# First filter block in two halves of its channels, identity loaded apart, k and v in four pieces each, and a new written-out order

## The chip, the cores and the metric

The kernel runs on one core of a Trainium2 chip. A time is device microseconds (us) of one execution; the median of several runs counts. One more execution was taken by the hardware profiler. Engines: PE (TensorE matmuls), PEld (its weight loads), DVE (VectorE), ACT (ScalarE), POOL (GpSimd), SP (SyncE, which issues most DMAs).

## The reference

S = 2048, D = 640, F = 1728, bf16 inputs and output.

```python
def _A_ref(q, k, v, shift_k, ssm_k, ssm_D):          # q is the layernorm of A_q
    k_shift = causal 4-tap filter of k along S, per channel
    kv = k_shift * v
    y = irfft(rfft(kv padded to 2S) * rfft(ssm_k padded to 2S))[:S]   # a long convolution
    y = y + kv * ssm_D
    return q * y
def _B_ref(x, w1, b1, w2):
    h = x @ w1 + b1
    return (h * tanh(softplus(h))) @ w2               # Mish
x = A_q
h = x + _A_ref(layernorm(x), A_k, A_v, ...)
out = h + _B_ref(layernorm(h), B_w1, B_b1, B_w2)
```

## The kernel before

The long convolution is done as a Fourier transform of length 4096 in two steps of matmuls, 128 and 16 points, for the filter (`h`) and for the data (`x`), a product of the two, and the two steps back. Channels stand in five chunks `dc` of 128; a step's work is cut into blocks of one pair of PSUM banks (1024 columns of f32), each evicted to SBUF by one copy on ACT or DVE.

Names of the steps, with their lines before:

- `d_kn{dc}` (L206) loads chunk `dc` of the filter, 128 channels by 2048, 512 KB. `consts` (L196, L197) loads, on ACT's queue, one table of 106 KB (identity 128 columns, first Fourier matrix `fcfs` 256, a mask and a small identity 40) and then the row of `ssm_D` ("D row", `Drow`).
- `pewarm` (L239) and `pewarm2` (L258) are matmuls on zeros, 512 columns each, eight and two. `drow` (L245) turns the D row into a column with five one-column matmuls, and `dadd` (L268) adds it to the first time step of the filter.
- `k1pe{dc}` (L295): 16 PE transposes of a filter chunk; `k1ev{dc}_{0,1}` two copies out of the bank.
- `s1pe_h_{dc}_{0..3}` (L280): first Fourier step of the filter, 16 matmuls a block; `s1ev_h` its eviction. `s1pe_x`, the same for the data.
- `gb` (L251) builds the second Fourier matrix from the table R (`d_R`, L208). `s2pe_h_*`, `s2pe_x_*` (L363): second step, `s2ev` its eviction.
- `d_k0`, `d_k1` (L225) load k in two halves of 1280 KB, `d_v0`, `d_v1` (L228) load v. `ktpe{dc}_{h}` (L314) transposes k, `ktev` evicts; `shpe{dc}` (L333) is the 4-tap filter as matmuls, `kv` (L341) multiplies by v on DVE.
- `d_sw` (L382) moves a filter spectrum block across partitions by DMA, 256 KB. `pr` (L412) multiplies the spectra on DVE. `i1pe` (L423, L424) and `i2pe` (L485) are the steps back, `i1ev` and `yev` their evictions.
- Rows: `ln1_T` (L464, L465) statistics of row tile T; `ln1s` (L470, L471 on POOL) and `ln1f` (L473) their finish; `lnx` (L535 on ACT); for the first two tiles `wbA`, `hA`, `bnA` (L500, L502, L503) and `wbB`, `hB`, `bnB` (L504, L506, L509 to L511); for later ones `wb`, `h`, `ln2` (L517, L519, L523); `dr` (L541); then a PE transpose (`trpe`, L549, evicted by `trev`) for tiles 0 and 1, a DMA transpose (`d_tr`, L553) for the others.
- `m1pe{u}_{fc}` (L573, L576), `mi` (Mish on ACT, L580), `m2pe{T}` (L597), `res` (L605, L616) and `d_o` (L600) are the feed-forward part, in row blocks `u` of 1, 1, 2, 4, 4, 4 tiles.

Every copy out of PSUM is recorded at one line, L185. Each engine runs its queue in order; the order over all engines is written out in `ORDER`, one word a step: name, engine, bank slot, and for DMAs on SP `@name`, the copy behind which the load is paced. Waits between steps follow from the data and the banks. The head of `ORDER` before:

```
d_kn0:sp consts:act small:pool warmset:dve d_kn2:sp pewarm:pe:0 tab:act d_kn4:sp d_kn1:sp d_kn3:sp d_k0:sp d_R0:sp
d_k1:sp d_R1:sp drow:pe:0 d_v1:sp pewarm2:pe:1 dadd0:dve k1pe0:pe:1 d_v0:sp k1ev0_0:dve k1ev0_1:dve s1pe_h_0_0:pe:3
```

Of the kernel before, what the change touches and what calls it, by code (L numbers as in the profile page):

```python
# [10 lines left out]
ALU = mybir.AluOpType  # L11
# [158 lines left out]
def plan(v):  # L170
# [24 lines left out]
    def e_consts(e):  # L195
        v.nc.scalar.dma_start(v.consts[:], v.dram["consts"])  # L196
        v.nc.scalar.dma_start(v.buf("Drow", [P, D])[0:1], v.A_D.rearrange("(o d) -> o d", o=1))  # L197
    g.op("consts", "act", e_consts, w=["consts", "Drow"], kind="consts")
# [6 lines left out]
    for dc in range(NDC):  # L205
        dma(f"d_kn{dc}", 524e3, lambda e, dc=dc: v.nc.sync.dma_start(v.buf("kn", [P, NDC, S])[:, dc, :], v.A_h[dc * P:(dc + 1) * P, :]), w=[("kn", dc)])  # L206
# [16 lines left out]
    if KPE:  # L223
        for h in range(2):
            dma(f"d_k{h}", 2048 * KC, lambda e, h=h: v.nc.sync.dma_start(  # L225
                v.buf("kna", [P, NT, KC])[:, 8 * h:8 * h + 8, :], v.A_k[0].rearrange("(p a) d -> p a d", a=NT)[:, 8 * h:8 * h + 8, 0:KC]), w=[("kna", h)])
    for h in range(2):
        dma(f"d_v{h}", 1.31e6, lambda e, h=h: v.nc.sync.dma_start(  # L228
            v.buf("v", [P, NT, D])[:, 8 * h:8 * h + 8, :], v.A_v[0].rearrange("(p a) d -> p a d", a=NT)[:, 8 * h:8 * h + 8, :]), w=[("v", h)])
# [6 lines left out]
    def e_pewarm(e):  # L236
        pw = bank(wrt)
        for i in range(8):
            v.nc.tensor.matmul(pw[:, 0:512], v.buf("warm", [P, 512])[:, 0:128], v.buf("warm", [P, 512]), start=True, stop=True)  # L239
# [6 lines left out]
    g.op("drow", "pe", e_drow, r=["Drow", "consts"], allocs=[drt], kind="drow")  # L246
# [9 lines left out]
    def e_pewarm2(e):  # L256
        for i in range(2):
# [3 lines left out]
    keep = g.op("pewarm2", "pe", e_pewarm2, r=["warm"], allocs=[wrt2], kind="pewarm2", after=[o for o in g.ops if o.name == "drow"])  # L261
# [4 lines left out]
    for i, (c0, c1) in enumerate(((0, 1), (1, 2), (2, 5))):  # L266
# [21 lines left out]
    def k1(dc, grp):  # L288
        rt = alloc(D2)
        kk = f"kk{dc % 4}"  # L290

        def pe(e):
            pk = bank(rt, BF16).rearrange("p (t d) -> p t d", t=NT)
            for t2 in list(range(1, NT)) + [0]:
                v.nc.tensor.transpose(pk[:, t2, :], v.buf("kn", [P, NDC, S])[:, dc, t2:S:NT], v.ident)  # L295
        g.op(f"k1pe{dc}", "pe", pe, r=[("kn", dc), "consts"], allocs=[rt], kind="k1pe", after=[keep])
        for h in range(2):
            g.op(f"k1ev{dc}_{h}", EV, lambda e, h=h: ev(
                e, v.buf(kk, [P, 64, NT, 2])[:, 32 * h:32 * h + 32], bank(rt, BF16).rearrange("p (t d m) -> p d t m", t=NT, m=2)[:, 32 * h:32 * h + 32]),
                w=[(kk, h)], uses=[rt], kind="evb", arg=1024)  # L300
        s1("h", dc, lambda: v.buf(kk, [P, 64, NT, 2]), kk, f"B{grp}", GRP_DG[grp][0])
# [6 lines left out]
    for h in range(2):  # L308
        for dc in range(KPE):
# [5 lines left out]
            g.op(f"ktpe{dc}_{h}", "pe", pe, r=[("kna", h), "consts"], allocs=[rt], kind="ktpe")  # L315
# [216 lines left out]
    def rows(T):  # L532
# [11 lines left out]
        if T < NEAR:  # L544
# [5 lines left out]
            g.op(f"trpe{T}", "pe", pe, r=[hc, "consts"], allocs=[rt2], kind="trpe")  # L550
# [264 lines left out]
```

## Time and profile before

| | us |
|---|---|
| median of 3 runs (228.5 to 228.97) | 228.62 |
| the profiled execution | 230.95 |
| its span, first to last instruction | 229.2 |
| PE, DVE, ACT, POOL busy in the span | 215.5, 149.0, 139.4, 28.1 |

Durations of single steps come from the profiled execution. A step that is "busy" overlaps its neighbours on the same engine by some tens of ns, so a queue's pace is read from start to start. The page's 40 slices are 5.73 us each. A PE that is shown busy need not run at its full rate: the pitch of its matmuls tells that. "Landing" of a DMA is the time from issue until its semaphore tells of the end.

### The profile page before, as it was taken

The page shows a single profiled execution, that of the slowest core. Times are in us where ns is not written, and L with a number is a line of the kernel's source. Part 1 is how long each engine was busy: PE and PEld are TensorE (multiplying, and loading weights), DVE is VectorE, ACT ScalarE, POOL GpSimd, SP SyncE. Part 2 cuts the span into 40 slices and gives each one's busy share as a digit, 9 for nine tenths or more (in the row PEclk, how much of TensorE's full clock was granted, in tenths as well). Part 3 has the DMA queues.
Part 4 walks back from the last instruction along what each step waited for, and adds up shares of the span by engine and source line. Part 5 has one row for each costly group of instructions (what it writes and reads, how often), then busy time and mean ns, then how long its engine had stood idle before and what let it go on. Part 6 is the DMA issues. An engine that isn't in the chain of part 4 may idle for free.

```text
span 229.2 us, 6927 instructions
## 1 busy us (share of the span) xinstructions
PE 215.5 (94%) x3016; PEld 162.4 (71%) x3021; DVE 149.0 (65%) x274; ACT 139.4 (61%) x200; POOL 28.1 (12%) x60
## 2 busy tenths in 40 slices
PE   6899998979888999999999999999999999999994
PEld 2798888868787899998978764447557444577773
DVE  0469999999999999999999999965001200004131
ACT  2159998847999999999939367781350466100000
POOL 2120000000010000221233443522000000000000
PEclk9999999999999999999999999999999999999999
DMA  6999604845665777788230423424000100002021
GB/s 204 402 370 374 247 3 97 182 100 139 157 152 138 209 202 219 227 228 257 83 86 4 104 39 87 87 59 60 30 0 29 57 3 0 0 0 85 33 80 35
DMA packets 19872, 27.87 MB, mean 122 GB/s; under 512 B 10881, under 2 KB 14978, under 8 KB 19330
## 3 DMA queue, kind: packets, MB, share of 16 engines
q1 hardware_dynamic: 19536, 27.32, 41.0%
q8 instruction: 23, 0.38, 0.7%
q10 hardware_dynamic: 146, 0.11, 0.5%
q0 software_dynamic: 160, 0.01, 0.2%
q14 instruction: 7, 0.06, 0.1%
HBM read 17.27 MB, written 2.62 MB: 87 GB/s over the span
## 4 chain that ended last, share of the span: by engine, by line
PE 65%; ACT 14%; DVE 12%; DMA 4%; issue 3%; ACTq 0%; DVEq 0%
PE banks L597 26%; PE banks L573 23%; ACT arena L185 14%; PE banks L280 4%; DVE arena L412 4%; PE banks L363 3%; DVE arena L185 3%; PE banks L295 2%; DMA arena<-arena 2%; PE banks L333 2%; DMA arena<-in_A_ssm_D_dram 2%; DVE st L464 2%; DVE arena L341 2%; PE banks L576 1%; PE banks L485 1%
## 5 line engine op out<-in xcount | busy, mean ns | idle before, releaser
L185 ACT CAST arena<-banks 128x1024 bf16<-128x1024 f32 (+3 forms) x93 | 79.9, 985 | 16.5 <-PE banks L280 11.7
L597 PE MATMUL banks<-arena 128*128 128x320 bf16 (+2 forms) x448 | 61.7, 299 | 0.0
L580 ACT ACTIVATE arena<-banks,b1s 128x512 bf16<-128x512 f32 (+2 forms) x84 | 41.5, 535 | 29.7 <-PE banks L573 29.1
L573 PE MATMUL banks<-arena 128*128 128x512 bf16 (+2 forms) x395 | 58.2, 305 | 0.6 <-DVE nmr L473 0.3
L597 PEld LDWEIGHTS <-arena 128*128 128x128 bf16 x448 | 43.2, 98 | 18.1
L573 PEld LDWEIGHTS <-arena 128*128 128x128 bf16 x400 | 33.1, 98 | 23.7 <-issue 0.6
L616 DVE TENSOR_TENSOR arena<-banks,arena 128x640 bf16<-128x640 f32 x15 | 12.2, 816 | 56.4 <-PE banks L597 52.6
L185 DVE CAST arena<-banks 128x1024 bf16<-128x1024 f32 (+1 forms) x27 | 30.4, 1158 | 2.0 <-PE banks L280 1.3
L280 PE MATMUL banks<-consts,arena 128*64 128x128 bf16 x640 | 23.3, 230 | 2.6 <-ACT arena L185 1.1
L363 PE MATMUL banks<-arena 128*128 128x64 bf16 (+1 forms) x512 | 22.5, 199 | 2.7 <-ACT arena L185 2.4
L280 PEld LDWEIGHTS <-arena 128*64 128x64 bf16 x640 | 20.3, 116 | 4.7 <-issue 2.7
L363 PEld LDWEIGHTS <-arena 128*128 128x128 bf16 x512 | 19.9, 98 | 4.7 <-issue 3.6
L412 DVE TENSOR_TENSOR arena<-arena 128x2048 bf16<-128x2048 bf16 x20 | 22.9, 1216 | 0.2 <-DMA arena<-arena 0.2
L535 ACT ACTIVATE arena<-arena,nmr,r1v 128x640 bf16<-128x640 bf16 x16 | 14.3, 930 | 8.7 <-DVE nmr L473 7.5
L423 PE MATMUL banks<-a,arena 128*128 128x128 bf16 x160 | 18.8, 219 | 0.7 <-ACT arena L185 0.6
L424 PE MATMUL banks<-a,arena 128*128 128x128 bf16 x160 | 18.7, 219 | 0.0
L424 PEld LDWEIGHTS <-arena 128*128 128x128 bf16 x160 | 15.6, 98 | 0.9 <-issue 0.8
L423 PEld LDWEIGHTS <-arena 128*128 128x128 bf16 x160 | 15.6, 98 | 0.6 <-DVE arena L412 0.3
L185 DVE COPY arena<-banks 128x1024 bf16<-128x1024 bf16 (+1 forms) x17 | 10.7, 658 | 5.3 <-PE banks L295 4.5
L464 DVE BATCH_NORM_STATS2 st<-arena 128x6 f32<-128x320 bf16 x32 | 13.8, 474 | 0.0
L341 DVE TENSOR_TENSOR arena<-banks,arena 128x512 bf16<-128x512 f32 x20 | 12.3, 681 | 0.7 <-PE banks L333 0.3
L523 DVE BATCH_NORM_STATS2 st<-arena 128x6 f32<-128x320 bf16 x28 | 12.3, 480 | 0.2
(60 smaller groups left out, 139.6 us busy)
## 6 DMA issues: line engine op xcount, KB each, us to landing
arena<-arena SPq DMA_DIRECT2D x20, 256.0 KB, 3.0
arena<-in_A_ssm_k_dram SPq DMA_DIRECT2D x5, 512.0 KB, 6.4
arena<-in_A_k_dram SPq DMA_DIRECT2D x2, 1280.0 KB, 13.1
arena<-in_A_v_dram SPq DMA_DIRECT2D x2, 1280.0 KB, 19.6
arena<-in_A_q_dram SPq DMA_DIRECT2D x8, 320.0 KB, 3.2
out_dram<-arena SPq DMA_DIRECT2D x15, 160.0 KB, 1.8
arena<-in_B_w_dram SPq DMA_DIRECT2D x5, 432.0 KB, 4.4
arena<-in_B_w_dram SPq DMA_DIRECT2D x3, 480.0 KB, 5.1
```

Source lines behind the costliest of these rows:

```text
L185: v.copy = v.nc.scalar.copy(o, i) if e == "act" else v.nc.vector.tensor_copy(o, i)
L280: v.nc.tensor.matmul(pz[64 * ri:64 * ri + 64, gl, :], lhs, v.fcfs[:, ri, :], start=True, stop=True)
L341: v.nc.vector.tensor_tensor(v.buf(f"kvb{dc}", [P, 64, NT, 2])[:, q * 16:(q + 1) * 16], bank(rts[h])[:, i * 512:(i + 1) * 512].rearrange("p ...
L363: v.nc.tensor.matmul(bank(rt)[:, fl * pitch:fl * pitch + nd], v.buf("G", [P, P, P])[:, f0 + fl, :], v.buf(f"B{grp}", [P, P, nd])[:, f0 + f ...
L412: v.nc.vector.tensor_tensor(kk, xx.unsqueeze(1).to_broadcast([P, 2, 16, 64]), kk, ALU.mult)
L423: v.nc.tensor.matmul(pz[:, gl, :], v.buf(f"KP{b}", [P, 16, P])[:, 8 * h + gl, :], v.a12[:, 0, :], start=True, stop=False)
L424: v.nc.tensor.matmul(pz[:, gl, :], v.buf(f"KPS{b}", [P, 16, P])[:, 8 * h + gl, :], v.a12[:, 1, :], start=False, stop=True)
L464: v.nc.vector.bn_stats(v.st1[:, T % 4, q, :], x(T)[:, q * 320:(q + 1) * 320])
L535: g.op(f"lnx{T}", "act", lambda e: v.nc.scalar.activation(lnx(), x(T), ACT.Identity, scale=v.r1v[:, T:T + 1], bias=v.nmr1[:, T:T + 1]), r= ...
L573: v.nc.tensor.matmul(ph[:, 0:w], w1[:, dc, fc * P:(fc + 1) * P], lt[:, dc, T0 * P:T0 * P + w], start=(dc == 0), stop=(dc == NDC - 1))
L580: g.op(f"mi{u}_{fc}", "act", lambda e, fc=fc, rt=rt, ww=ww: v.nc.scalar.activation(ub()[:, fc, 0:ww], bank(rt)[:, 0:ww], ACT.Mish, bias=v. ...
L597: v.nc.tensor.matmul(bank(rt)[:, q * 512:q * 512 + b - a], lhs, w2()[:, wc, a:b], start=(fc == 0), stop=(fc == NFC - 1))
```

## The change

- The identity (128 columns of `consts`) is loaded by a DMA of its own, first on ACT's queue; then the D row, then the remaining 296 columns.
- `kn` chunk 0 is loaded in two halves of 64 channels. Its transposes become two groups, `k1pe0_0` and `k1pe0_1`, of 16 transposes on 64 rows each, in one bank each, with one copy each. For this chunk the D row is added behind the copy, on one partition (`dk0_0`, `dk0_1` on DVE), in place of the first `dadd`.
- `pewarm` has seven matmuls for eight, `pewarm2` one for two, and stands behind `pewarm` in place of `drow`.
- k and v are loaded in four pieces each (640 KB). These loads, R's and `a12` are paced behind copies, where they stood unpaced at the head.
- `ORDER` is another one throughout.

```diff
-        v.nc.scalar.dma_start(v.consts[:], v.dram["consts"])
         v.nc.scalar.dma_start(v.buf("Drow", [P, D])[0:1], v.A_D.rearrange("(o d) -> o d", o=1))
+        v.nc.scalar.dma_start(v.consts[:, 128:424], v.dram["consts"][:, 128:424])
+    g.op("ident", "act", lambda e: v.nc.scalar.dma_start(v.consts[:, 0:128], v.dram["consts"][:, 0:128]), w=["ident"], kind="ident")
...
-    for dc in range(NDC):
+    for h in range(2):
+        dma(f"d_kn0_{h}", 262e3, ... kn[64 * h:64 * h + 64, 0, :] <- A_h[64 * h:64 * h + 64, :] ...)
+    for dc in range(1, NDC):
...
-        for h in range(2):
-            dma(f"d_k{h}", 2048 * KC, ... [:, 8 * h:8 * h + 8, :] ...)
-    for h in range(2):
-        dma(f"d_v{h}", 1.31e6, ... [:, 8 * h:8 * h + 8, :] ...)
+        for h in range(4):
+            dma(f"d_k{h}", 1024 * KC, ... [:, 4 * h:4 * h + 4, :] ...)
+    for h in range(4):
+        dma(f"d_v{h}", 655e3, ... [:, 4 * h:4 * h + 4, :] ...)
...
-        for i in range(8):          # pewarm
+        for i in range(7):
-        for i in range(2):          # pewarm2
+        for i in range(1):
...
+        if dc == 0:
+            for h in range(2):
+                rt = alloc(D1)
+                def pe(e, h=h, rt=rt):
+                    pk = bank(rt, BF16).rearrange("p (t d) -> p t d", t=NT)
+                    c = slice(64 * h, 64 * h + 64)
+                    for t2 in range(NT):
+                        v.nc.tensor.transpose(pk[:, t2, :], v.buf("kn", [P, NDC, S])[c, 0, t2:S:NT], v.ident[c, c])
+                g.op(f"k1pe0_{h}", "pe", pe, r=[("kn", (0, h)), "ident"], ...)
+                g.op(f"k1ev0_{h}", EV, ...)
+                g.op(f"dk0_{h}", "dve", ... kk[0:1, half h, 0, :] += Drow[0:1, 64 * h:64 * h + 64] ...)
```

The head of the new order, and where its k, v and R loads stand:

```
ident:act d_kn0_0:sp small:pool warmset:dve consts:act d_kn0_1:sp pewarm:pe:0 d_kn1:sp tab:act d_kn4:sp d_kn3:sp d_kn2:sp
pewarm2:pe:0 k1pe0_0:pe:1 k1pe0_1:pe:2 k1ev0_0:dve drow:pe:3 dk0_0:dve k1ev0_1:act s1pe_h_0_0:pe:1 dadd0:dve s1pe_h_0_1:pe:0
s1ev_h_0_0:act k1pe1:pe:2 s1ev_h_0_1:dve k1ev1_0:act d_R0:sp:@s1ev_h_0_0 dk0_1:dve diag:dve s1pe_h_0_3:pe:1 s1ev_h_0_3:act
s1pe_h_1_1:pe:0 k1ev1_1:dve s1pe_h_1_3:pe:2 s1ev_h_1_1:act ...
d_k1:sp:@s1ev_h_1_1 d_v0:sp:@k1ev3_0 d_R1:sp:@s1ev_h_1_0 d_k0:sp:@k1ev4_0 d_v1:sp:@s2ev_h_0_1 d_v3:sp:@s1ev_h_4_3
d_k2:sp:@s1ev_h_3_2 d_k3:sp:@s2ev_h_0_4 d_v2:sp:@ktev1_0 d_a12:sp:@ktev0_0
```

Around the end of the products the DVE queue is `... pr_8_1 pr_8_0 ln1_1 ln1_0 ln1f_0 i1ev9_0 wbA0 hA0 bnA0 wbB0 hB0 bnB0 wbA1 yev2_1 dr0 ln1_2 trev0 ln1_3 hA1 bnA1 wbB1 ln1f_2 hB1 bnB1 yev2_0 wb3 dr1 wb2 h3 trev1`, where before it was `... pr_9_1 yev1_0 yev0_0 wbA1 wbA0 hA0 hA1 bnA1 bnA0 wbB0 hB0 bnB0 wbB1 hB1 bnB1 dr0 ln1_2 dr1 trev0 ln1_7 ln1_8 ln1_3 ln1_5 trev1`, with `ln1_0` and `ln1_1` some 30 us ahead, among the evictions of `s2pe_x`. `d_x2` and `d_x4` (row tiles 4, 5, 8, 9 of A_q) stand behind `yev2_0` and `yev2_2`.

## The prediction

> **What bounds the kernel now.** I read the page first, then the chain of waits, then busy time by stretches and the timeline.
>
> ```profile
> PE 215.5 (94%) x3016; PEld 162.4 (71%) x3021; DVE 149.0 (65%) x274; ACT 139.4 (61%) x200; POOL 28.1 (12%) x60
> DVE  0469999999999999999999999965001200004131
> ACT  2159998847999999999939367781350466100000
> ```
>
> The 65% of DVE is an average: it is full in slices 4 to 26 (17 to 150 us) and nearly idle after. So three stages are costed apart: to the last product (L412), from there to the second row block (L573), and the dense matmuls behind.
>
> ```profile
> 8.20:94.30 86.10, 78.33 (x1973) 72.26 (x1972) 80.38 (x100) 74.56 (x87) 5.19 (x9) 1.00 0.67 195
> 94.30:108.80 14.50, 13.97 (x204) 12.94 (x201) 13.69 (x39) 14.50 (x28) 2.48 (x5) 1.00 0.82 242
> ```
>
> Columns: stretch, length, busy PE, PEld, DVE, ACT, POOL. In stage 1 DVE is busy 80.4 of 86.1 us: evictions and products pace it. In stage 2 DVE is busy 13.7 of 14.5. Behind 108.8 PE hardly waits (from 109 to 229.2 it is busy 116.5 of 120.2 us, and the rest is nearly all the last 4.2 us), its work is the same in both versions, and each us at 108.8 is a us at the end.
>
> The head, from the chain of waits, then the timeline:
>
> ```profile
> 1.12 4.14 DMA arena<-in_A_ssm_D_dram
> 5.32 0.28 PE banks L245 x5
> 5.60 0.97 PE banks L258 x2
> 6.57 1.72 PE banks L295 x16
> 8.31 0.70 DVE arena L185
> 9.06 3.62 PE banks L280 x64
> ```
> ```profile
> 1.18 3.59 PE L239 MATMUL banks<-arena 128*128 128x512 bf16 x8 [1.18 <-DVE dumm L201]
> 5.32 0.28 PE L245 MATMUL banks<-consts,arena 1*128 1x1 bf16 x5 [0.54 <-DMA arena<-in_A_ssm_D_dram]
> ```
>
> The D row's load holds `drow`, then come `pewarm2`, `k1pe0`, one DVE copy, and the first filter block at 9.06. Last, L295 alone, by stretches (length, busy PE and PEld with counts, clock, DMA share, GB/s):
>
> ```profile
> 12.60:13.40 0.80, 0.79 (x8) 0.79 (x9) 1.00 0.97 319
> 13.40:14.20 0.80, 0.80 (x15) 0.80 (x14) 1.00 1.07 185
> ```
>
> 8 transposes in 0.8 us, then 15: PE runs at half speed until 13.4, though the clock column reads 1.00 throughout. L280 says the same: 64 in 3.62 us (0.90 per block of 16) up to 12.7, against 32 in 0.90 (0.45 a block) between 16.8 and 17.7.
>
> **Part by part.** The profiled execution took 230.95, its span 229.2 and 1.75 around it; the median of the runs is 228.62. The terms are made against the 229.2 span and carried over to the median as differences.
>
> *Head.* `pewarm` starts at 1.18, one per 0.427 us (the L239 weight loads stand at 2.01, 2.44, 2.86). Seven and `pewarm2`'s one keep PE busy to 1.18 + 8 x 0.427 = 4.60. `k1pe0_0` waits for the identity (the 106 KB table landed 3.9 us after 0.72, at 4.6; 32 KB of it, first on the same queue, is no later) and for half of `kn` 0 (the first whole one took 4.4 us, to 5.1; half its packets end earlier, 4.4 to 4.7). So it starts near 4.7 with a gap of about 0.1. Its 16 transposes move 64 columns, not 128: between 0.053 each (half of 1.72/16) and 0.107; I take 0.06, as the 64-column L363 matmuls also run at half the L295 pitch. That is 1.0, then 0.2 for the last write, 0.70 for the copy, 0.16 for `dk0_0` (the L268 add) and 0.1 of handoff: first block at 6.85 instead of 9.06, 2.2 earlier (bounds 1.4 and 2.4). The second half hides behind the copy; `drow` has 0.28 in the same shadow, and its D row (5.27 before) stands ahead of the big table now. `fcfs`, the 76 KB rest, must land before 6.85: the first 106 KB took from about 2.0 to 4.6, so 76 KB behind 4.5 take 1.9, to 6.4; if later, that is the loss. ACT's third issue (0.37) hides before its first copy at 6.8; so do five more issues on SP.
>
> 2.2 us at half speed are 2.4 blocks; later a block costs what ACT and DVE need together, 1/(1/0.90 + 1/1.15) = 0.50. Worth: 1.2.
>
> *The clock.* Before, the 3.59 us stretch from 1.18 did not raise it, nor the one from 5.32 to 8.29; the stretch from 9.06, with one gap of 0.2, did, 4.3 us on. The new stream stands from 1.18 to beyond 10 with gaps near 0.1, so the same 4.3 gives 5.5; I take 5.5 to 8.5. The Trainium skill, "TensorE: Matmul & The Clock Gate", Part 1, says that a free-running window of about 3.4 us must be busy throughout; by that the stretch from 1.18 raises the clock between 4.6 and 8.0; that 3.59 us did not suffice before agrees, as it would have had to meet a window almost exactly. From 6.85 the new PE queue holds five blocks and one `k1pe` up to 13.1 at half speed (5 x 0.90 + 1.72 = 6.2); at full speed 3.3, but their copies on ACT (five at 0.90 = 4.5) then bind: 4.5 in place of 6.2 to 6.5. Worth: 2.0 (bounds 0 and 3.0).
>
> *DVE in stage 1.* Its list loses `ln1_0` and `ln1_1` (2 x 1.0) and four filter copies (4 x 0.60), gains two `ktev` (1.2), one block eviction (1.1), one of s2 (1.0) and the small adds (0.3): -0.8, and I take 0.7. ACT takes four filter copies and gives up as many. Worth: 0.7. So stage 1: -1.2 - 2.0 - 0.7 = -3.9.
>
> *Paced loads.* `d_k0` now follows `k1ev4_0`; `ktpe2_0` stands about four ACT evictions (4 x 0.90 and handoffs, 3.8) behind it, and all of PE's queue behind that.
>
> ```profile
> arena<-arena SPq DMA_DIRECT2D x20, 256.0 KB, 3.0
> arena<-in_A_q_dram SPq DMA_DIRECT2D x8, 320.0 KB, 3.2
> arena<-in_B_w_dram SPq DMA_DIRECT2D x3, 480.0 KB, 5.1
> ```
>
> 640 KB: 4.2 on the line through the first two, 6.8 in proportion to the third, which queued behind its like. A piece goes out each 1.8 us, so nearer the first: 4.2, 0.4 late; 0.3 after slack (bounds 0 and 2.5). By "DMA: Bandwidth & Descriptors", Anatomy of one DMA, of the Trainium skill (2.0 us and 436 GB/s) it would be an estimated 3.5, on time: 0.3 less. v's last piece has six ACT evictions, 5.4 us, to `kv1_1`.
>
> *Stage 2, the price.* In the chain of waits:
>
> ```profile
> 94.30 1.15 DVE arena L185
> 108.66 0.16 DVE nmr L473
> 108.82 0.21 PE banks L573
> ```
>
> Before, DVE went from 94.30 to 108.57 (`trev1`), and PE took `m1pe1` at 108.82: 14.5. The new DVE list behind its last product, in steps of the timeline: `ln1_1`, `ln1_0` 2.0; then `ln1f_0` waits for POOL (L470 0.26, L471 0.73, handoffs: 1.1) and costs 0.16; `i1ev9_0`, behind four PE groups of 0.9, 0.7 more wait and 1.15; row 0 (L500, L502, L503: 1.4; L504 to L511: 1.2); `wbA1` 0.4, `yev2_1` 0.65 (by size from 0.94 for 768 columns); `dr0`, `ln1_2`, `trev0`, `ln1_3` 2.8; row 1's rest 2.4; `yev2_0`, `wb3`, `dr1`, `wb2`, `h3`, `trev1` 2.65. Sum 16.6, and 0.2 to PE: 16.8. That is +2.3: three statistics left (`ln1_7`, `ln1_8`, `ln1_5`, 3.0) but two came from stage 1, with two waits (1.8) and work of rows 2 and 3. Without the waits +0.5.
>
> Behind it the margins stay: `d_tr2` (2.6 us) is covered by `m2pe0`, half of the 7.6 us of L597's 56. `d_x2` and `d_x4`, sent late, land 3.2 us on, before `ln1_5` and `ln1_8`. Work added on PE: 16 short transposes, about 0.5 at full speed, in the copy's shadow; removed: two warm matmuls that filled idle time.
>
> Sum: -3.9 + 0.3 + 2.3 = -1.3, so 228.62 - 1.3 = 227.3. With the unknown sizes this case spans 226.3 to 228.1.
>
> **Rivals.** *The clock one window later*, near 10: for it, `drow` and the 64-row transposes load PE lightly; against it, the 0.2 gap behind 12.4 was no hindrance before. Half of the 2.0 is lost: 228.3. *Late loads*: a piece as slow as the 480 KB rows stalls `ktpe2_0` by 1.3 more: 228.6; for it, k's two halves took 13.1 us to land behind other loads; against it, pieces now go out one by one, and 256 KB alone take 3.0. *Slower, the clock no earlier than before*: identity or half filter land after about 5.1, so PE has the old half-us gap (0.54 above) at 4.6 and the clock rises at 12 or later; for it, the whole filter landed at 5.1 and the table at 4.6; against it, only half of each is waited for. Then the head brings 1.2, DVE 0.7, and stage 2's 2.3 with the loads' 0.3 outweighs them: +0.7, 229.3. It decides from a rise at about 11 on. This is also the case in which the parting of identity and filter does nothing.
>
> **How the numbers follow.** Main case 0.50, later window 0.17, late loads 0.11, no earlier clock 0.22. 0.2% (0.46 us) is about what a measurement of this kernel can tell. Faster than 228.16: 0.46 + 0.07 + 0.03 + 0 = 0.56. Within: 0.03 + 0.07 + 0.04 + 0.03 = 0.17. Slower: 0.01 + 0.03 + 0.04 + 0.19 = 0.27. The range reaches from the main case's better end to a late clock with a small stall: 226.2 to 229.5.
>
> **What would show it.** Right: first L280 block near 6.9; 16 transposes in about 1 us rather than 1.7 before 9; last L412's end near 90.7; 16 to 17 us from there to `m1pe1`, with DVE idle for POOL ahead of `ln1f_0`. Wrong: L280 after 7.6, half-speed pitch beyond 11, PE idle before `ktpe2_0`, or PE idle above 1 us behind the second row block.

## The result, and the profile after

The changed kernel takes 230.97 us (median of 20 runs, 229.28 to 231.67), the kernel before 228.75 on the same chip (20 runs, 228.21 to 231.43): ratio 1.0082, 95% interval 1.0061 to 1.0102. It is 2.2 us slower; 1.3 us faster was forecast. Its profiled execution took 230.45 with a span of 228.7 (before: 230.95 and 229.2), so the two profiled executions stand the other way round than the medians. That contradiction is the first thing to explain.

The page of after, busy time and its slices (5.72 us each):

```profile
PE 215.8 (94%) x3035; PEld 162.2 (71%) x3035; DVE 148.6 (65%) x275; ACT 141.7 (62%) x200; POOL 28.0 (12%) x60
DVE  0588888999999999699999999795000231011121
ACT  2589897669999999999949418796600006621000
```

DVE's row has eights up to slice 7 where it had nines from slice 4 on, and a 6 in slice 17, right behind the last product. The stretches from the first filter block to the last product (now L433), and from there to the second row block (now L594); columns as in the prediction:

```profile
7.05:92.01 84.96, 77.13 (x1959) 70.42 (x1956) 77.54 (x92) 75.49 (x86) 2.58 (x5) 1.00 0.73 203
92.01:108.68 16.67, 15.90 (x217) 14.55 (x217) 14.35 (x42) 16.37 (x27) 4.42 (x8) 1.00 0.76 225
```

Stage 1 has 2.1 us less DVE work (77.5 busy; from 9.06 to 94.30 before it was 79.6) and is nearly as long as it was: 84.96 for 85.24. Stage 2 is 16.67 for 14.50, as forecast. The head, PE's timeline:

```profile
1.18 3.17 PE L242 MATMUL banks<-arena 128*128 128x512 bf16 x7 [1.18 <-DVE dumm L202]
4.14 0.63 PE L261 MATMUL banks<-arena 128*128 128x512 bf16 x1
4.71 2.19 PE L302 MATMUL banks<-consts,arena 64*128 64x64 bf16 x32
6.83 0.29 PE L248 MATMUL banks<-consts,arena 1*128 1x1 bf16 x5
7.05 1.92 PE L283 MATMUL banks<-consts,arena 128*64 128x128 bf16 x32
```

The half transposes (L302) start where they were expected and the first block (L283) at 7.05, but its 32 matmuls take 1.7 us: half speed. Two waits of the new order, the first on PE ahead of `ktpe2_0`, the others on DVE behind the last product:

```profile
25.49 1.07 PE L335 MATMUL banks<-consts,arena 128*128 128x128 bf16 x16 [1.14 <-DMA arena<-in_A_k_dram]
```
```profile
95.30 0.16 DVE L494 SCALAR_TENSOR_TENSOR nmr<-mv,r1v 128x2 f32<-128x2 f32 x1 [1.25 <-POOL r1v L492]
95.93 1.22 DVE L185 CAST arena<-banks 128x1024 bf16<-128x1024 f32 x1 [0.47 <-PE banks L445]
```

### The profile page after: what moved, and what is told of

Read it like the earlier page. It is cut to its first block, busy times and chain, and to the rows that moved or that the text cites. A ratio compares the mean times of both kernels' runs of the same rounds, so it can differ in the third digit from the quotient of the medians.

```text
span 228.7 us, 6987 instructions
## 1 busy us (share of the span) xinstructions
PE 215.8 (94%) x3035; PEld 162.2 (71%) x3035; DVE 148.6 (65%) x275; ACT 141.7 (62%) x200; POOL 28.0 (12%) x60
## 4 chain that ended last, share of the span: by engine, by line
PE 55%; ACT 17%; DMA 3%; DVE 3%; issue 2%; ACTq 0%; SPq 0%
PE banks L618 26%; PE banks L594 23%; ACT arena L185 15%; DMA arena<-arena 2%; DVE arena L433 2%; DMA arena<-in_B_w_dram 2%; PE banks L354 1%; ACT arena L556 1%; ACT arena L601 1%; PE banks L597 1%; PE banks L384 1%; PE banks L506 1%; PE banks L283 1%; DVE arena L362 1%; DVE arena L637 0%
## 5 line engine op out<-in xcount | busy, mean ns | idle before, releaser
L185 ACT CAST arena<-banks 128x1024 bf16<-128x1024 f32 (+2 forms) x91 | 80.3, 994 | 6.1 <-PE banks L384 3.0
L594 PE MATMUL banks<-arena 128*128 128x512 bf16 (+2 forms) x400 | 58.6, 306 | 0.2 <-ACT arena L601 0.2
L594 PEld LDWEIGHTS <-arena 128*128 128x128 bf16 x400 | 33.2, 98 | 24.0 <-issue 0.4
L185 DVE CAST arena<-banks 128x1024 bf16<-128x1024 f32 (+2 forms) x29 | 31.3, 1108 | 4.9 <-PE banks L283 2.7
L283 PE MATMUL banks<-consts,arena 128*64 128x128 bf16 x640 | 23.3, 225 | 1.4 <-ACT arena L185 1.1
L433 DVE TENSOR_TENSOR arena<-arena 128x2048 bf16<-128x2048 bf16 x20 | 23.0, 1218 | 0.4 <-ACT arena L185 0.2
L283 PEld LDWEIGHTS <-arena 128*64 128x64 bf16 x640 | 19.8, 113 | 3.4 <-issue 1.1
L185 DVE COPY arena<-banks 128x1024 bf16<-128x1024 bf16 (+1 forms) x15 | 9.5, 654 | 5.6 <-PE banks L302 4.8
```

Of the source, the lines that this page charges most:

```text
L185: v.copy = v.nc.scalar.copy(o, i) if e == "act" else v.nc.vector.tensor_copy(o, i)
L283: v.nc.tensor.matmul(pz[64 * ri:64 * ri + 64, gl, :], lhs, v.fcfs[:, ri, :], start=True, stop=True)
L433: v.nc.vector.tensor_tensor(kk, xx.unsqueeze(1).to_broadcast([P, 2, 16, 64]), kk, ALU.mult)
L594: v.nc.tensor.matmul(ph[:, 0:w], w1[:, dc, fc * P:(fc + 1) * P], lt[:, dc, T0 * P:T0 * P + w], start=(dc == 0), stop=(dc == NDC - 1))
```

## The experiments

Lines in the kernels named a_... are those of after, in b_... those of before, unless a fence shows others. Where a ratio is given, it is to the kernel before on the same chip; the kernel after itself stands at 1.0082 (above) and 1.0127 (below), so only what leaves 1.006 to 1.015 is a difference.

### Which execution had been read: both kernels again

No edit. The theories in these first four texts are CLOCK, by which the time hangs on when PE's clock rises, and QUEUES, by which it hangs on the new order of the queues.

> The kernel before, unchanged, profiled a second time. Theory CLOCK (in most executions before, PE's rate rises far earlier than the 13.4 us of the profile that was read, and the new head delays it): the half-speed pitch of the matmuls ends before 9 us, the span is 226.5 to 227.5 us, and the stages behind the head are as long as they were. Theory QUEUES (the new order costs the time behind the head): the rate rises near 13 again, and the span is near 229.

> The changed kernel, unchanged, profiled a second time. CLOCK: the rate rises at 10 to 13 us, and the span follows the rise by about 0.3 us for each us: 228.5 to 229.7. QUEUES: the rise may come at any time, and a span near 229.2 comes from waits behind 30 us that the first profile did not show, above 1 us more of PE idle between 30 and 110.

b_look: 228.71 (227.93 to 230.43, 12 runs), ratio 1.0007 [0.9986, 1.0028]. a_look: 231.66 (231.35 to 231.8, 4 runs), ratio 1.0127 [1.0106, 1.0147]. The unchanged kernel before, PE's timeline, in an execution with a span of 227.5:

```profile
4.91 0.29 PE L245 MATMUL banks<-consts,arena 1*128 1x1 bf16 x5
5.12 0.74 PE L258 MATMUL banks<-arena 128*128 128x512 bf16 x2
5.70 1.17 PE L295 MATMUL banks<-consts,arena 128*128 128x128 bf16 x16
7.65 1.53 PE L280 MATMUL banks<-consts,arena 128*64 128x128 bf16 x48 [0.78 <-DVE arena L185]
```

and its two stages:

```profile
7.65:92.58 84.93, 77.05 (x1972) 70.58 (x1972) 79.84 (x99) 74.80 (x87) 5.27 (x9) 1.00 0.68 201
92.58:107.08 14.50, 13.91 (x200) 12.93 (x201) 13.69 (x40) 14.44 (x28) 2.48 (x5) 1.00 0.77 247
```

The same program: 16 transposes in 1.17 us where the execution read for the prediction took 1.72, 48 matmuls of L280 in 1.53 where 64 took 3.62. PE is at full speed from about 5.5 on, the first block starts at 7.65 and not at 9.06, and the second row block at 107.08 and not at 108.80. With 1.75 us around the span, a median of 228.6 to 228.75 means a span near 227.0: b_look (229.24, half a us above its median) is nearer the usual case, and the execution with the rise at 13.4 a late one. Of the head start of 2.0 us only 0.6 is new. Nor is all of the other 1.4 the clock's: the D row's load let `drow` start at 4.91 here and at 5.32 there, 0.4 us apart.

In a_look (span 229.9) PE was up at 4.1 already and lost it again. Busy PE by stretches (clock is the third figure from the end):

```profile
4.10:7.40 3.30, 2.85 (x41) 2.36 (x41) 0.89 (x2) 0.13 (x1) 0.65 (x1) 1.00 1.00 281
7.50:10.90 3.40, 3.40 (x48) 3.15 (x46) 1.81 (x4) 1.79 (x2) 0.24 (x1) 0.50 1.03 378
```

Of the 2.85 us busy in the first stretch, 2.36 are the half transposes. So in these two executions the clock of the new head rose late (10.0 in the profile of after, where L316's pitch falls) or fell back. The clock column shows the fall, but reads 1.00 before the first rise as well, where only the pitch of the matmuls tells half speed from full.

### The clock and the head start: warm matmuls

```diff
b_w71, in pewarm and pewarm2 of before
-        for i in range(8):
+        for i in range(7):
-        for i in range(2):
+        for i in range(1):
a_w12, in pewarm of after
-        for i in range(7):
+        for i in range(12):
```

> The kernel before with the warm matmuls of the changed one, seven and one in place of eight and two; nothing else changed. The wide matmul taken from the first group filled time in which PE waits anyway, the one behind it stands on the head's path, 0.43 us at half speed. CLOCK: the rate rises later than before in most executions, 1 to 2 us slower than the kernel before (229.5 to 231). QUEUES: 0 to 0.4 us faster (228.3 to 228.8).

> The changed kernel with twelve matmuls in the first warm group in place of seven: 2.1 us more of wide matmuls ahead of the first half filter, so the first block begins near 9.2 in place of 7.05. CLOCK: the wide stretch of 5.5 us raises the rate by 8 us at the latest; the later start and the earlier rate about cancel, 230.5 to 231.2, and its executions spread less than those of the changed kernel. QUEUES: the 2.1 us are lost, of which the copies behind give back at most half: 232 or more.

b_w71: 229.82 (227.94 to 230.95, 12 runs), ratio 1.0038 [1.0010, 1.0067]; in its profile PE stood 0.62 us ahead of `drow`, the first block came at 8.29 at half speed, the last product ended at 93.84 (b_look 92.58). In the old order, then, the one execution with a rise at 13.0 ended stage 1 1.3 us after the one with a rise at 5.4. That the missing warm matmuls bring such executions on is likely from the spread of the runs, but only one of them was profiled. a_w12: 231.0 (230.53 to 231.95, 6 runs), ratio 1.0106 [1.0085, 1.0127]. Its clock was up before the first block (6.7), which started at 9.01, 1.6 us later than in a_look; yet it was no slower on the same chip. From the first block to the last product it took 84.51. Its last product ended at 93.52, in an execution that was the slowest of its six: later than in a_look (93.20), whose clock had fallen back, and 1.5 us later than in a_fill (92.00, below), which had an early clock and started 2.0 us sooner. So these profiles show no rule for how much of a head start reaches the end.

The clock alone, with nothing else changed ahead of stage 2, came by chance with a_fill (below), the same program as after up to the last product. The first block by stretches, after and then a_fill:

```profile
7.00:8.70 1.70, 1.65 (x32) 1.65 (x32) 1.00 1.03 410
```
```profile
7.00:8.00 1.00, 0.96 (x32) 0.92 (x32) 1.00 1.04 414
```

a_fill is at full speed 5 us earlier. Its products start 0.6 us earlier (68.06 for 68.68), and its last one ends at 92.00 for 92.01. DVE's timeline of a_fill says where the 0.6 went:

```profile
87.37 4.63 DVE L433 TENSOR_TENSOR arena<-arena 128x2048 bf16<-128x2048 bf16 x4 [0.78 <-DMA arena<-arena]
```

The last four products wait for a swap load, `d_sw9_0`, which landed at 87.34 there and at 87.36 in after, where DVE stood 0.18 us for it. The load had left 0.6 us earlier there (82.80 for 83.41) and took 0.6 longer to land (4.55 for 3.94). So in this pair a rise 5 us earlier was worth 0.6 us at the first product and nothing at the end of stage 1.

### The head alone, and all but the head

```
b_head     code of after but k and v in two pieces; ORDER of before behind s1pe_h_0_0; ahead of it
           ident d_kn0_0 consts d_kn0_1 pewarm(7) pewarm2(1) k1pe0_0 k1pe0_1 k1ev0_0 drow dk0_0 k1ev0_1 dk0_1
a_oldhead  code of before but k and v in four pieces; ORDER of after behind s1pe_h_0_0; ahead of it
           d_kn0 consts pewarm(8) drow pewarm2(2) dadd0 k1pe0 k1ev0_0 k1ev0_1
```

> The kernel before with the new head alone: identity loaded apart, chunk 0 in two halves of its channels with `dk0_0` and `dk0_1`, seven and one warm matmuls, `drow` behind the transposes; k and v stay in two pieces each, all early loads go out at once, and the order behind the first filter block is that of before. Theory HEAD (the first filter block starts 0.3-0.6 us earlier than in the usual execution of before, 7.05-7.4 for 7.65, and hands that on to the end one for one; the clock's rise is worth little): 0.2 to 0.7 us faster than before, 228.0-228.5. Theory CLOCK (the 64-row transposes count as idle for the clock, which rises at 8.5 to 11 instead of 5.5 or falls back): the head's gain is eaten up, 0 to 1.0 us slower than before, 228.7-229.7, and half-speed pitch seen behind 8.

> The kernel after with the head of before: one table load, chunk 0 loaded and transposed whole, eight and two warm matmuls, `drow` and the first add ahead of the transposes; k and v in four pieces, the paced loads and the whole new order behind the first filter block stay. It is what b_head leaves out. Theory PARTS (the head costs about what b_head showed, 0.3%, and the order the rest): 0.4 to 0.8 us faster than the kernel after, 229.6-230.6, ratio to before 1.004-1.008, first filter block at 7.5-7.8 with the clock up near 5.5. Theory ORDER (the head is worth nothing here either way, since the end of stage 1 hangs on the loads and products): within 0.3 us of the kernel after, 230.7-231.6.

b_head: 229.57 (228.71 to 230.66, 12 runs), ratio 1.0033 [1.0015, 1.0051]. The first block starts 0.8 us earlier than in b_look, at full speed, and the last product ends at 92.49 for 92.58. PE's timeline:

```profile
6.85 2.52 PE L283 MATMUL banks<-consts,arena 128*64 128x128 bf16 x64
10.36 2.21 PE L316 MATMUL banks<-consts,arena 128*128 128x128 bf16 x32 [0.99 <-DMA arena<-in_A_ssm_k_dram]
```

The four blocks of chunk 0 are done earlier, and then PE stands 0.99 us for chunk 1's load, which the old order sends behind two others. What is gained ahead of a load is lost to it. a_oldhead: 232.06 (231.53 to 233.42, 6 runs), ratio 1.0137 [1.0111, 1.0163]: not faster than after, against PARTS; its first block started at 8.39. No gain from the head can be told in either order; in the old one it is 0.3% to the bad.

### Whole transposes

```diff
a_whole, in k1 of after, for chunk 0 too
-  for h in range(2): ... transpose(pk[:, t2, :], kn[c, 0, t2:S:NT], v.ident[c, c])
+  transpose(pk[:, t2, :], kn[:, 0, t2:S:NT], v.ident)      # both half loads awaited
- k1pe0_0:pe:1 k1pe0_1:pe:2
+ k1pe0:pe:2
```

> The kernel after, with chunk 0 transposed by 16 whole transposes (128 rows, 128 columns) into one buffer in place of 32 half ones; the two half loads, the identity apart and the two row adds `dk0_0` and `dk0_1` stay. Theory NARROW (the half transposes cost as much each as whole ones, and load PE too lightly to raise or hold its clock): PE starts its first filter block at 6.4-7.2 (half transposes: 7.05-7.37), spends 1.0 us less on transposes ahead of 9 us, the clock rises before 8 and does not fall back, the time falls by 0.4 to 1.2 us from the kernel after, to 229.8-230.6. Theory CHANCE (the rise of the clock differs from execution to execution whatever PE does in the first 8 us): rise anywhere from 4 to 13, the time within 0.4 us of the kernel after.

233.46 (233.27 to 234.37, 5 runs), ratio 1.0200 [1.0155, 1.0246]. NARROW fails, but not for its reason: the two half loads together ended later (6.05) than the one whole load had (5.1 in the profile of before, 5.4 in b_look), and PE stood for them.

```profile
6.05 1.90 PE L298 MATMUL banks<-consts,arena 128*128 128x128 bf16 x16 [1.27 <-DMA arena<-in_A_ssm_k_dram]
8.97 1.92 PE L283 MATMUL banks<-consts,arena 128*64 128x128 bf16 x32 [0.80 <-DVE arena L271]
```

With these gaps the clock rose near 12.6. It says nothing on the price of narrow transposes; that is read below from after and a_fill.

### The statistics of rows 0 and 1

```diff
a_ln and a_whole_ln, in ORDER of after and of a_whole
- pr_8_0 ... ln1_1 ... ln1_0 ... ln1s_0 ... ln1f_0
+ c_b1 ln1_1 ln1_0 ln1s_0 ... pr_8_0 ln1f_0
b_lnlate, in ORDER of before
- s2pe_x_1_4 ln1_0 ... s2ev_x_1_4 ln1_1 ... s2ev_x_0_5 ln1s_0 ... i1ev4_1 ln1f_0 ... pr_8_0 lnx1 ... pr_9_1 i1pe8_0 lnx0
+ pr_8_0 ... pr_9_1 ln1_1 ln1_0 ln1s_0 ln1f_0 i1pe8_0 ... i1ev8_0 lnx1 lnx0
```

> The kernel after, with `ln1_1`, `ln1_0` and `ln1s_0` taken from behind the last product to behind `c_b1` (near 64 us), and `ln1f_0` left behind the last product. Theory WAIT (the 2.2 us that stage 2 lost are these statistics and the two waits that stand behind them, and stage 1 has room for them because PE and ACT pace it at that place): stage 2 falls from 16.67 to 14.2-15.2, the last product ends at most 0.8 us later, the time falls by 1.1 to 1.8 us from that of the kernel after (near 231), to 229.2-229.9. Theory FULL (DVE is full in stage 1 too, so what is taken out of stage 2 is paid in stage 1): stage 2 falls by 2, the last product ends 1.6 to 2.0 us later, the time stays within 0.5 us of the kernel after, 230.5-231.5.

> The kernel after with both: whole transposes of chunk 0, and `ln1_1`, `ln1_0`, `ln1s_0` behind `c_b1`. If WAIT and NARROW both hold, the two gains add: 1.5 to 3.0 us below the kernel after, 228.0-229.5, about level with the kernel before or just under it. If only one holds, 229.2-230.6. If neither, within 0.5 us of the kernel after.

> The kernel before, with `ln1_1`, `ln1_0`, `ln1s_0` and `ln1f_0` moved from their places in stage 1 to behind the last product `pr_9_1`, and `lnx1` and `lnx0` behind `i1ev8_0` on ACT: that part of the new order alone. Theory WAIT: stage 2 grows from 14.5 to 16.2-17.2, the last product ends 0 to 1.0 us earlier, the time rises by 1.0 to 2.0 us to 229.8-230.8 (ratio to before 1.004-1.009). Theory FULL: stage 2 grows the same, but the last product ends 1.6 to 2.0 us earlier, and the time is within 0.5 us of before.

a_ln: 233.17 (231.12 to 234.13, 6 runs), ratio 1.0163 [1.0116, 1.0211]. a_whole_ln: 237.35 (235.14 to 239.70, 6 runs), 1.0323 [1.0271, 1.0374]. b_lnlate: 234.54 (231.84 to 234.93, 6 runs), 1.0199 [1.0143, 1.0255]. All three lose, in both directions. The stages of a_whole_ln and DVE's timeline behind its last product:

```profile
8.64:96.73 88.09, 78.39 (x1956) 71.24 (x1956) 79.24 (x97) 76.11 (x87) 3.26 (x6) 1.00 0.69 190
96.73:113.38 16.65, 15.92 (x216) 14.51 (x217) 12.28 (x35) 16.18 (x27) 3.39 (x6) 1.00 0.73 216
```
```profile
95.51 1.22 DVE L419 TENSOR_TENSOR arena<-arena 128x2048 bf16<-128x2048 bf16 x1
96.65 0.15 DVE L480 SCALAR_TENSOR_TENSOR nmr<-mv,r1v 128x2 f32<-128x2 f32 x1
100.65 1.22 DVE L185 CAST arena<-banks 128x1024 bf16<-128x1024 f32 x1 [3.85 <-PE banks L431]
```

Against a_whole (85.60 and 16.91), stage 1 is 2.5 us longer and stage 2 is 0.3 shorter. (In a_ln stage 1 was as long, 88.06, but its clock also fell at 70.6, for 3.4 us; a_whole_ln had no such fall, so the reading is taken from it.) With the statistics gone, DVE stands 3.85 us until PE has done `i1pe8_0`, `i1pe8_1`, `i2pe0_0` and `i1pe9_0`. Last product to that copy: 3.92 us here, 3.92 in after. The 2.0 us of statistics and the wait for POOL lie in PE's shadow; they are not what stage 2 pays for.

b_lnlate is the other half. Its stage 1 took 85.03 us without these 2.0 us (b_look 84.93), its stage 2 19.51:

```profile
93.27:112.78 19.51, 15.62 (x203) 14.05 (x201) 15.82 (x47) 16.08 (x29) 4.37 (x8) 0.91 0.61 188
99.00:102.30 3.30, 3.30 (x24) 2.69 (x22) 2.81 (x6) 2.40 (x4) 0.00 (x0) 0.50 0.28 66
```

PE stood 3.42 us up to 97.82 for a bank that DVE was to empty behind the statistics, and then ran at half speed for 3.4. So in these executions 2.0 us taken out of DVE's list in stage 1 shortened it by nothing, and 2.0 put into it cost 2.5. ACT had no gap at the end of that stage: 38 copies in 31.73 us from 59.30, as in b_look from 58.76 (31.73 too), so relief of DVE may have had nothing to shorten there. WAIT and FULL were each half right, and neither foresaw PE's floor.

### Stage 2 of the new order

```
a_fill   after: ln1_2 between ln1_0 and ln1f_0; ln1_3 ln1s_2 between ln1f_0 and i1ev9_0
a_st2    a_fill, and wb3 wb2 h3 behind trev1, lnx3 lnx2 behind mi0_0, dr1 trpe1 behind ln2s_1
a_st2b   after: ln1_2 behind ln1s_0; dr1 trpe1 behind ln2s_1, trev1 behind m1pe0_10, i2pe2_2 behind mi0_3;
         lnx3 lnx2 behind mi0_0, wb3 wb2 h3 ln2_3 behind lnx2; other bank slots for trpe1 and i2pe2_2
```

> The kernel after, with two statistics of stage 2 moved into DVE's waits behind the last product: `ln1_2` between `ln1_0` and `ln1f_0` (where DVE stands 1.25 us for POOL), `ln1_3` and `ln1s_2` between `ln1f_0` and `i1ev9_0` (where it stands 0.47 us for PE). Nothing leaves stage 2. Theory SHADOW (behind the last product PE needs 3.9 us for `i1pe8_0`, `i1pe8_1`, `i2pe0_0` and `i1pe9_0` before DVE can take `i1ev9_0`, whatever DVE does meanwhile; from there to `trev1` DVE is full, and only its list counts): stage 2 falls from 16.67 by 2.0 less the 0.5 by which `ln1_3` delays `i1ev9_0`, to 15.0-15.5, and the time falls by 1.0 to 1.7 us from the kernel after, to 229.3-230.0. Theory LATE (m1pe1 waits for something else, the row sums on ACT or PE's queue): stage 2 stays above 16.2 and the time within 0.5 us of the kernel after.

> The kernel a_fill, and besides: `wb3`, `wb2` and `h3` (1.4 us of rows 2 and 3) moved from ahead of `trev1` to behind it, `lnx3` and `lnx2` on ACT from among the first row block's Mishes to behind `mi0_0`, and `dr1` and `trpe1` right behind `ln2s_1`. Theory SHADOW: DVE's list from `i1ev9_0` to `trev1` falls by 3.4 us in all, stage 2 to 13.4-14.4, `m1pe0` takes 4.1-4.6 us instead of 5.6, and the time falls by 2.0 to 3.2 us from the kernel after, to 227.8-229.0, level with the kernel before or under it. A part may come back later, as PE waits for rows 2 and 3 ahead of the third row block (up to 1 us). Theory LATE: within 0.7 us of a_fill.

> The kernel after, with row 1 set ahead of rows 2 and 3 in stage 2: `ln1_2` in DVE's wait for POOL behind the last product; `dr1`, `trpe1` and `trev1` right behind `ln2s_1` (in other PSUM banks), `i2pe2_2` behind `mi0_3`; `wb3`, `wb2`, `h3` and `ln2_3` behind `lnx2`, and `lnx3` and `lnx2` behind `mi0_0` on ACT. Theory ROW1 (the new order loses in stage 2 because row 1's work and rows 2 and 3's are mixed ahead of `trpe1`: `m1pe0` takes 5.6 us in place of 4.1 and PE stands for `dr1`): `m1pe1` starts at 106.8-107.8 in place of 108.7, stage 2 takes 14.8-15.8; the end falls by 0.5-1.5 us, or by less where the third row block then waits for rows 2 and 3. Theory SUM (DVE, ACT and PE are each full between the last product and the second row block, so another of them holds `m1pe1`): `m1pe1` moves by less than 0.5 us.

a_fill: 231.47 (230.46 to 233.80, 6 runs), ratio 1.0135 [1.0097, 1.0173]; stage 2 16.61. The waits behind the last product were filled and DVE had 2.0 us less to do later, but:

```profile
106.43 0.49 DVE L538 TENSOR_TENSOR arena<-arena 128x640 bf16<-128x640 bf16 x1 [0.93 <-ACT arena L556]
106.84 0.44 DVE L562 TENSOR_SCALAR arena<-arena,mv,r 128x640 bf16<-128x640 bf16 x1
```

`wb3` (L538) stands ahead of `dr1` (L562) in DVE's queue and waits for `lnx3`, which ACT reaches behind six Mishes at 105.4 (105.2 in after). Part of the gain was lost before that, where `ln1_3` delayed `i1ev9_0` by 0.5 us. a_st2 has two steps too early for what they read (rows 2 and 3 take `lnx`'s buffers before ACT writes them, `trpe1` a bank before its Mish), so its waits are not those of the order meant; 232.24 us, ratio 1.0163 [1.0123, 1.0203], decides nothing. a_st2b, the same idea in a sound order: 233.9 (233.51 to 234.08, 5 runs), ratio 1.0203 [1.0160, 1.0247]. `m1pe1` began at 109.28, later than in after, for PE then waited for ACT (0.65 and 1.09 us) and for rows 2 and 3 (1.32 us ahead of the third row block). SUM holds: from the last product to the second row block PE, DVE and ACT are so close that relief on one, or a new order of rows, shows the next.

### The paced load of k

```diff
a_k0, in ORDER of after
- d_v0:sp:@k1ev3_0 ... d_k0:sp:@k1ev4_0
+ d_k0:sp:@k1ev3_0 ... d_v0:sp:@k1ev4_0
```

> The kernel after, with `d_k0` and `d_v0` changing places: `d_k0` follows `k1ev3_0` (it goes out near 15.2) and `d_v0` follows `k1ev4_0` (near 20.4). Theory STALL (PE stands 1.14 us ahead of `ktpe2_0` because `d_k0` lands 5.1 us after its issue, and all behind it is late by that): `d_k0` lands at 19-21, PE has no idle time ahead of `ktpe2_0`, products start 0.6-1.2 us earlier, and the time falls by 0.4-1.2 us from the kernel after (near 231), to 229.8-230.6. Theory SWAPS (what stage 1 gains ahead of the products is lost to the swap loads: in a_fill products started 0.6 us earlier and then stood 0.78 us for `d_sw9_0`, which landed at 87.3 in both): the stall goes, the products start earlier, and the last one still ends at 91.9-92.2; time within 0.3 us of the kernel after.

231.43 (230.67 to 232.07, 8 runs), ratio 1.0091 [1.0054, 1.0127]. PE's and DVE's timelines of a_k0:

```profile
24.45 1.07 PE L335 MATMUL banks<-consts,arena 128*128 128x128 bf16 x16
```
```profile
88.08 4.63 DVE L433 TENSOR_TENSOR arena<-arena 128x2048 bf16<-128x2048 bf16 x4 [0.54 <-DMA arena<-arena]
```

PE's wait of 1.14 us is gone from `ktpe2_0`, but one of 1.12 for a later piece of k has come up behind it, where after has none:

```profile
34.09 2.18 PE L335 MATMUL banks<-consts,arena 128*128 128x128 bf16 x36 [1.12 <-DMA arena<-in_A_k_dram]
```

So the wait was moved and not cured. The last product ends at 92.71 (clock at half from 7.3 to 10.7, as in a_look, where it ended at 93.20 with a wait of 1.70), and not at the 91.9 to 92.2 that SWAPS gave. The time is that of after, as SWAPS had it (STALL gave 229.8 to 230.6); but what the paced loads cost by themselves stays open, and the part of the swap load, for which DVE stood 0.54 us, is not shown either.

### Room in the old stage 2

```
b_defer    before: ln1_2 behind trev0; ln1_7 ln1_8 ln1_5 behind ln1f_2; ln1s_2 behind ln1_3
b_defer2   the same, but ln1_7 ln1_8 ln1_5 ln1_13 behind ln2_3
b_defer3   ln1_2 behind trev0; ln1_7 ln1_8 behind ln1f_2; ln1_5 ln1_13 ln1_11 behind dr3; d_tr2 behind dr2
```

> The kernel before, with `ln1_2` moved behind `trev0`, and `ln1_7`, `ln1_8` and `ln1_5` behind `ln1f_2` (which follows `trev1`); `ln1s_2` stands right behind `ln1_3`. SHADOW says of this kernel that DVE's list ahead of `trev0` and PE's transposes are the chain, and that what stands between `trev0` and `trev1` hides under `m1pe0` (4.1 us of PE): `m1pe0` starts 0.3 to 0.9 us earlier, 101.8-102.4 where the last look at before had 102.70, `m1pe1` follows it without a wait, and the time falls by 0.2 to 0.9 us, to 227.8-228.5. Theory LATE (PE's start of `m1pe0` hangs on copies of ACT): no change within 0.3 us.

> The kernel before, with `ln1_2` behind `trev0`, and `ln1_7`, `ln1_8`, `ln1_5` and `ln1_13` behind `ln2_3` rather than ahead of rows 2 and 3 (in b_defer three of them stood ahead of `wb2`, and PE then stood ahead of the third row block, which began at 118.57 as in before). Theory ROOM (the 1.5 us that b_defer gained at `m1pe1` go on to the end if rows 2 and 3 are not held up): `m1pe1` at 105.4-105.8, the third row block at 117.0-117.6 in place of 118.6, the time 0.8 to 1.4 us below before: 227.3-227.9. Theory LATER (another wait takes it: rows 4 to 7, or the loads of w2): the third row block at 118.0 or later, or PE idle behind it, and the time within 0.4 us of before.

> The kernel before, with `ln1_2` behind `trev0`, `ln1_7` and `ln1_8` behind `ln1f_2` (in b_defer2 DVE stood 2.3 us there for `lnx2`), `ln1_5`, `ln1_13` and `ln1_11` behind `dr3` (in b_defer2 they stood ahead of `dr2` and `dr3`, and PE stood 3.05 us for `d_tr2`), and `d_tr2` right behind `dr2`. Theory ROOM (what m1pe1 gains goes on to the end once nothing is put ahead of rows 2 and 3): `m1pe1` at 105.2-105.8, the third row block at 116.8-117.5 without a wait, the time 0.8 to 1.5 us below before, 227.2-228.0. Theory LATER (another wait takes it): the third row block at 118 or later and the time within 0.4 us of before.

b_defer: 229.67 (229.13 to 230.22, 12 runs), ratio 1.0031 [1.0016, 1.0047]. b_defer2: 233.34 (231.68 to 234.59, 6 runs), 1.0175 [1.0119, 1.0230]. b_defer3: 231.52 (230.33 to 233.12, 6 runs), 1.0108 [1.0070, 1.0147]. In b_defer and b_defer2 the second row block starts at 105.57 and 105.24, 1.5 and 1.8 us before b_look's 107.08. Of this 0.7 and 1.0 came before the edit: the last product ended at 91.90 and 91.56 there, at 92.58 in b_look, on the same order. Stage 2 itself took 13.7 us in all three (93.31 to 106.99 in b_defer3) for 14.50, 0.8 less. The third row block (L573) on PE's timeline, b_defer, b_defer2, b_defer3:

```profile
118.57 7.27 PE L573 MATMUL banks<-arena 128*128 128x256 bf16 x65 [0.93 <-DMA arena<-arena]
```
```profile
120.58 5.66 PE L573 MATMUL banks<-arena 128*128 128x256 bf16 x35 [3.05 <-DMA arena<-arena]
```
```profile
118.89 3.44 PE L573 MATMUL banks<-arena 128*128 128x256 bf16 x30
122.93 0.71 PE L573 MATMUL banks<-arena 128*128 128x256 bf16 x5 [0.60 <-ACT arena L580]
```

b_look has it at 118.64 without a wait. Each time the gain was given back at the next place where a moved statistic was needed: ahead of `d_tr2` and `d_tr3`, or on ACT within the row block. In b_defer2 the wait of 3.05 us also brought the clock down behind it (last section). LATER holds; none of the versions beats the kernel before.

## Why the prediction was wrong, step by step

*Carrying differences over to the median* is the step that failed first. The sum was made against an execution of 230.95 us and taken off a median of 228.62. The two differ by 2.3 us, and b_look shows that much of that is the late clock, with a D row 0.4 us later, and what they do to the head: 1.7 us up to the end of stage 1. A change can't gain that from a median whose executions mostly lack it (b_look's span of 227.5 lies near the 227.0 that the median means). Of the head's 2.2 us, 1.4 were of this kind (9.06 to 7.65). Taken off the execution that was read, the same sum gives a span of 227.9 and a time of 229.65, so of the 3.7 us between 227.3 and 230.97 this step makes 2.3. Most of the rest is the second failed step, the gains in stage 1: it was to end at 90.7 and ended at 92.01 in after, at 93.20 in a_look.

*The clock's 2.0.* A rise between 5.5 and 8.5 was forecast; it came at 10.0 in one profiled execution of after, and in another it was up by 4.1 and down again from 7.5 to 10.9. The later rise was a rival, at half the worth. But the worth was the larger error: beside after, a_fill had the early clock, was 0.6 us ahead at the first product and level at 92.0.

*The head's 1.2.* The first block came at 7.05 for 6.85: right. The 16 half transposes took 1.0 us: right at half speed. At full speed they took as long, so the second sixteen cost 1.0 and not 0.5. Handing 1.2 us on to the end was not borne out: in the old order b_head lost its 0.8 to the load of chunk 1. In the new order a_w12 started 1.6 us later than a_look and was no slower, but ended stage 1 1.5 later than a_fill, so what of it reaches the end there stays open.

*DVE's 0.7.* The list did shrink (77.5 us busy for 79.6), and stage 1 did not. The premise "evictions and products pace it" took 80.4 busy of 86.1 for a limit. b_lnlate took 2.0 us out of the old order for nothing. The relief did come through in the stretch of the products, b_look and then after, and was lost ahead of it (61.63 us from the first block to the first product for 60.46):

```profile
68.11:92.58 24.47, 23.11 (x377) 21.37 (x375) 24.08 (x24) 24.47 (x31) 1.29 (x3) 1.00 0.70 196
68.68:92.01 23.33, 21.21 (x368) 19.58 (x365) 22.96 (x22) 23.32 (x28) 0.36 (x1) 1.00 0.78 198
```

ACT, the fourth of the busy columns, has no gap in either. The chain of waits runs over its copies from 60 to 83 us in after and from 62 to 76 in b_look, then over a swap load, and only then over DVE's last products. The last of those copies and the load, after and then b_look:

```profile
79.54 3.85 ACT arena L185 x4
83.41 3.94 DMA arena<-arena
```
```profile
75.16 1.09 ACT arena L185
76.27 4.78 DMA arena<-arena
```

So ACT's copies are the likely limit of the last third of stage 1. No run relieved ACT alone, so this is a reading and not shown.

*The paced loads' 0.3.* PE stood 1.14 us in after and 1.70 in a_look; `d_k0` took 5.1 and 5.6 us to land, not 4.2. The wait is inside the bounds given (0 to 2.5), and in a_look about what the rival "late loads" came to (0.3 and 1.3 more; by its rows, 5.1 for 4.2, it should have said 0.9). a_k0 only moved the wait, so what it cost is not shown. The estimate of 3.5 from the Trainium skill's "DMA: Bandwidth & Descriptors", Anatomy of one DMA, was further off than the 4.2; the page fits it to loads that GpSimd issues, and these go out on SP.

*Stage 2's 2.3* measured 2.17, with the waits foreseen (1.25 for 1.1, 0.47 for 0.7). The number is right and its account only in part: the statistics and waits in it run beside 3.9 us of PE work, and DVE's list is one of three near-equal limits (a_fill, a_st2b).

*Behind 108.7* nothing was to change: 120.0 us from the second row block to the span's end, 120.4 in b_look. Right within 0.4.

Sum, of spans, from b_look to after: head -0.6, stage 1 0.0, stage 2 +2.2, rest -0.4, together +1.2; to a_look -0.3, +0.9, +2.2, -0.4, together +2.4. The medians differ by 2.2. (The executions of b_look and after lie half a us above and below their medians, which is why this pair shows 1.2 only.) So what was right was the price, and what was wrong was every gain against it. The rival on the slower side had the right outcome by a mechanism that did not decide: it called for a rise at 11 or later, and a_fill is slow with a rise at 5.0. What holds stage 1 at 84.0 to 85.8 us in every order tried but a_ln's and a_whole_ln's stays open as a single cause. Seen are waits for chunk 1, for `d_k0` and for `d_sw9_0`, and ACT without a gap in its last third. On one and the same order up to the last product, stage 1 took 84.0 to 85.2 us in b_look and the three b_defer versions, so single profiles can't settle less than about a us of it.

## What to carry to other kernels

Compare the profiled execution's own time with the median before reading it: where they differ by more than the effect sought, find what in the trace is unusual, and don't book its absence as a gain. A stage in which PE, DVE and ACT are each about 90% busy (77.1, 77.5 and 75.5 of 85.0 us here) need not get shorter by relief to one of them, and still gets longer by a load on one: here, in single executions, 2.0 us taken out of DVE brought nothing and 2.0 put in cost 2.5. Such an average also hides an engine that has no gap in part of the stage, as ACT in the last 32 us of this one. Work that moves into a later stage must be weighed against what that stage waits for anyway, and work that is put off costs time where its result is next needed.

## What the runs showed of the hardware

In five profiles PE's clock fell back to half, each time for 3.4 us. In three of them the stretch just before held little PE work. From b_defer2, busy PE behind the comma, clock third from the end:

```profile
117.80:121.20 3.40, 0.62 (x6) 0.56 (x7) 3.33 (x12) 1.55 (x2) 1.86 (x4) 1.00 0.62 145
121.30:124.60 3.30, 3.30 (x18) 2.27 (x16) 3.16 (x9) 2.71 (x6) 0.00 (x0) 0.50 0.01 2
```

So the wait of 3.05 us on PE cost, by estimate, another 1.7 us (half of 3.4) behind it. By the Trainium skill, "TensorE: Matmul & The Clock Gate", Part 1, the clock is judged by free-running windows of 3413 ns, and falls back after an idle one; the length agrees with these stretches. What counts as idle is wider here: the clock of b_lnlate fell with PE busy 1.08 of 3.40 us, that of a_ln with 1.49 of 3.30, and in the new head that of a_look with 2.85 of 3.30, of which 2.36 were 64-row transposes, and that of a_k0 with 3.23 of 3.41. It is no rule for that head: after, a_fill and b_head have the same 32 transposes and their clock did not fall.

The half transposes kept one pitch at both clocks. L302 by stretches, after and then a_fill, which differ by the clock from 5.0 on:

```profile
4.70:6.80 2.10, 2.09 (x32) 2.07 (x32) 1.00 1.04 319
```
```profile
4.70:6.80 2.10, 2.10 (x32) 2.10 (x32) 1.00 0.98 287
```

The whole ones of before took 0.107 us each at half speed and 0.062 within a run at full speed (16 in 1.17 us, the last one's drain included). Halving rows and columns thus saves PE nothing once the clock is up.
